# Two chained attentions on one core: PSUM as one eight-bank tile, the end of the second attention on pairs of units, and another order of instructions

## The chip, the core and the metric

The kernel runs on one core of a Trainium2 chip. The metric is device time in microseconds (us), the median of several runs. A core has TensorE (PE, matrix products, with weight loads shown apart as PEld), VectorE (DVE), ScalarE (ACT), GpSimd (POOL) and SyncE (SP, which here issues every transfer). Each engine runs its own instructions in the order in which the program issued them and waits on semaphores for the others. Matmul results land in PSUM, eight banks of 512 fp32 values in each of 128 partitions; inputs and other results live in SBUF.

## The reference

The first attention has 4 batches, 8 heads, 768 positions and a head size of 64, with a bias by distance; a query sees the first 8 keys and the last 96. Its output, (4, 768, 512), is the input x of a second layer: four experts, each a causal attention of head size 64 on all 768 positions, two of which are chosen per token and weighted.

```python
scores = scale * q @ k.T                       # 1 / sqrt(64)
keep = (pos_k < 8) | (0 <= pos_q - pos_k < 96)
scores = where(keep, scores - slope[h] * dist, -1e9)
x = softmax(scores) @ v                        # heads side by side: (4, 768, 512)

logits = x @ w_gate                            # (4, 768, 4)
topk = the 2 largest; w = exp(their logits); w /= w.sum()
for e in range(4):
    a = softmax(causal(scale * (x @ wq[e]) @ (x @ wk[e]).T))
    out += w[e if chosen else 0] * (a @ (x @ wv[e]) @ wo[e])
```

## The kernel before

The work is cut into 24 units: unit u is 128 positions, number ri = u % 6 of batch u // 6. Positions are loaded for two units at once (q and k, 512 KB each) and for one unit (v, 256 KB). The steps of a unit have short names, which a table called `ORDER` lists in the order in which they are issued; it is the order on every engine, SP included. In the table `s0-5:0` is step s0 of unit 5 in PSUM slot 0, and a star picks the second of the engines that a step may run on.

The steps of the first attention: `ldq`, `ldk`, `ldv` load (SP). `cq`, `ck`, `cv` cast to fp16 (POOL, for the first unit ACT and DVE). `tq`, `tk` transpose (PE, L591 and L596) and `eq`, `ek` copy the result to SBUF (DVE). `s0`, `s1` are the scores of four heads each, transposed (PE, L630); `x0`, `x1` their exponentials (ACT, L634), 1024 elements to a partition, or 512 for the first unit of a batch; `m0`, `m1` the product with the stored factors M of bias and mask (DVE, L639). `z0`, `z1` multiply by V (PE, L647 and L650), with a column of ones in V that gives the sum of each row; `r0`, `r1` are its reciprocals (DVE, L661), and `n0`, `n1` the normalised rows in fp16 (DVE, L663). The first eight positions of a batch are copied into each unit's blocks by `kp` (POOL) and `vp` (an SP transfer that waits for z0 and z1).

Then come the projections: `tx`, `ex` transpose x (PE L679, DVE), `pq` multiplies by wq and wk (PE, L689) and `eqk` copies out (DVE or ACT), `pv` multiplies by wv and w_gate (PE, L695), `ev` copies the values out (ACT or DVE). The routing: `xr` is the exponential of the logits (ACT, L708), `mx` the sorted largest (DVE, L711), `wr` keeps those of the two chosen experts and sums them (DVE, L712), `zi` is the reciprocal of the sum (DVE, L715).

The second attention: `s20`, `s21`, `s22` scores (PE, L727) and `x20` to `x22` exponentials (ACT, L731), in parts of up to four blocks; `af` cuts the diagonal block (POOL, L739). Its end, called for each unit: `y2` multiplies by the values (PE, L751); `rz` takes the reciprocals of the sums (DVE, L757); `cw` multiplies weights, `zi` and `rz` (DVE, L758); `n2` scales (DVE, L761); `tz`, `ez` transpose (PE L769, DVE); `po` multiplies by wo (PE, L774); `eo` copies out (ACT or DVE); `so` stores (SP, L783). L384 is the copy helper of all casts and copies.

PSUM is cut into named slots: two of two banks each for scores, `s0` and `s1`, and four of one bank, `w0` to `w3`, for all else. SBUF buffers are rings: three for blocks of q and k, four units for the rest. The weights are loaded once (`ld-q`, `ld-k`, `ld-v`, `ld-o`, 512 KB each, and `ld-g`, 8 KB) and cast (`w-q` and so on). `warm` runs 24 matmuls on zeros at the start. At the end `good0` to `good2` test that all sums are in range, `total` adds the tests up on PE, `flag` copies the count out, and a branch on it, with `hint` just ahead of it, leads to a general path that these inputs don't take.

Of the kernel before, what the change touches and what calls it, by code (L numbers as in the profile page):

```python
# [8 lines left out]
F32 = mybir.dt.float32  # L9
# [7 lines left out]
P = 128  # L17
N_G, N_L = 8, 96
N_WARM = 24

ORDER = """
ident nil ldq-0 warm:2 ldk-0 ident32 ldq-2 dg ldk-2 iota d mask ldv-0 d0 d1 M-1-1 ldq-4 cq-0 ck-0
ld-k M-0-0 M-1-0 tk-0:3 cq-2 tq-0:1 ek-0 ld-q M-0-1 V1one* eq-0 tq-2:2 perm kg-0 s0-0:1 ldv-1 eq-2
s1-0:0 ck-2 x0-0 x1-0 m0-0 kp-0 V2one ld-g s0-1:1 m1-0 s1-1:0 tk-2:3 x1-1 kp-1 cv-0 ek-2 vg-0 z1-0:2
x0-1 r1-0 s0-2:0 n1-0 cq-4 z0-0:0 x0-2 r0-0 vp-0 m1-1 tq-4:1 ld-v m0-2 n0-0 eq-4 ldk-4 tx-0:0 w-q*
s1-2:1 ldv-2 kp-2 w-k* cv-1 w-g ex-0 z1-1:1 m0-1 x1-2 r1-1 z0-1:3 pq-0:0 m1-2 vp-1 w-v* ldv-3 r0-1
n1-1 s1-3:1 ldq-6 n0-1 x1-3 eqk-0 tx-1:3 pv-0:2 ld-o ck-4 s20-0:0 xr-0 mx-0 s0-3:1 ex-1 x20-0 ev-0*
x0-3 wr-0 cv-2 tk-4:3 kp-3 z0-2:0 ek-4 af-0 zi-0 m0-3 y2-0:2 z1-2:1 s0-4:0 cv-3 vp-2 r1-2 r0-2
s1-4:1 rz-0 x0-4 ldk-6 pv-1:3 cw-0 kp-4 n2-0 ldq-8 n0-2 pq-1:2 x1-4 cq-6 n1-2 ldv-6 ones mx-1 ldk-8
m1-3 eqk-1* tq-6:1 tx-2:0 m1-4 w-o z0-3:2 ex-2 s20-1:1 r0-3 s0-5:0 m0-4 pq-2:0 xr-1 x0-5 wr-1 eq-6  # L30
ck-6 ev-1 n0-3 s1-5:0 eqk-2* z1-3:2 x20-1 vp-3 m0-5 tk-6:1 ldv-4 r1-3 tz-0:0 x1-5 pv-2:3 ldk-10 ek-6
af-1 n1-3 kg-6 s0-6:1 s1-6:0 ez-0 x0-6 m1-5 tx-3:2 po-0:0 x1-6 ldq-10 kp-6 m0-6 y2-1:1 ldq-12 xr-2
eo-0 cq-8 ex-3 s21-2:1 s0-7:0 rz-1 x21-2 mx-2 pq-3:2 zi-1 ldv-7 cw-1 x0-7 cv-6 ev-2* wr-2 tq-8:0
ck-8 n2-1 eqk-3* s1-7:1 eq-8 s20-2:0 x1-7 z0-6:1 tz-1:3 m1-6 tk-8:2 cv-4 r0-6 ez-1 x20-2 z1-6:0 n0-6
s20-3:1 vg-6 r1-6 z1-4:1 n1-6 po-1:3 ck-10 vp-6 ek-8 ldv-5 s21-3:0 eo-1 r1-4 tx-6:0 n1-4 pv-3:2
x20-3 kp-7 ex-6 z0-4:3 m0-7 tk-10:1 xr-3 ev-3 vp-4 cq-10 pq-6:0 r0-4 x21-3 n0-4 ek-10 tx-4:3 af-2
zi-2 ldk-12 mx-3 s0-8:1 ex-4 s1-8:0 cq-12 ldq-14 x0-8 eqk-6 pq-4:3 m1-7 so-1 tq-12:1 eqk-4* cv-7
wr-3 tq-10:0 eq-12 x1-8 s21-4:1 eq-10 cv-5 z0-7:1 z1-7:2 x21-4 r0-7 kp-8 s20-4:0 m1-8 vp-7 z0-5:0
ldv-8 z1-5:3 x20-4 r1-7 n0-7 s22-4:1 r0-5 n1-7 y2-2:1 ck-12 r1-5 x22-4 n0-5 tx-7:2 ldk-14 n1-5
s1-9:0 s20-6:1 rz-2 tx-5:3 x20-6 cw-2 ldv-9 ex-7 tk-12:0 ldq-16 x1-9 ex-5 cq-14 s0-9:1 ek-12 pq-5:2  # L40
x0-9 zi-3 n2-2 kp-9 af-4 pv-5:3 eqk-5* m0-8 s0-10:1 tq-14:1 xr-5 af-3 mx-5 x0-10 wr-5 pq-7:2 cv-8
eq-14 ev-5 m1-9 s21-5:0 eqk-7* s1-10:1 m0-10 z1-8:3 x21-5 z0-8:1 kp-10 r1-8 tz-2:2 kg-12 y2-3:0
ck-14 r0-8 vp-8 ez-2 x1-10 n1-8 ldv-10 pv-4:2 rz-3 n0-8 ldk-16 po-2:3 cw-3 ldv-12 cv-9 tx-8:1 n2-3
eo-2 s22-5:0 so-0 ex-8 s1-11:1 xr-4 ev-4 m0-9 tz-3:0 tk-14:3 x22-5 cq-16 mx-4 pq-8:1 ez-3 ek-14
x1-11 m1-10 s1-12:0 po-3:0 x1-12 af-6 eqk-8 z1-9:3 eo-3 s0-12:1 m1-12 s20-5:0 x0-12 wr-4 z0-9:1
pv-6:0 ck-16 zi-4 x20-5 r1-9 vp-9 r0-9 n1-9 y2-4:2 ldq-18 zi-5 n0-9 xr-6 so-2 ev-6 s21-8:1 rz-4
s0-11:0 af-5 mx-6 ldk-18 x21-8 wr-6 tx-9:3 tq-16:1 cw-4 ldv-11 x0-11 kp-12 ex-9 cv-10 tk-16:0 n2-4
eq-16 s20-8:1 ldv-13 s20-7:0 x20-8 m1-11 tz-4:2 pq-9:3 ez-4 ek-16 x20-7 af-8 z0-10:1 po-4:2 m0-11
eqk-9* y2-5:0 cq-18 r0-10 eo-4 n0-10 s1-13:1 rz-5 s21-9:0 cw-5 x1-13 cv-12 z1-10:1 n2-5 tq-18:2
vp-10 r1-10 m0-12 tz-5:3 x21-9 z1-12:0 ldq-20 n1-10 s0-13:1 ez-5 so-3 pv-7:1 kp-13 eq-18 ck-18 x0-13  # L50
ldk-20 po-5:3 r1-12 mx-7 ev-7* tx-10:2 xr-7 s1-14:0 zi-6 eo-5 wr-7 s0-14:1 vg-12 x1-14 zi-7 z0-12:1
ex-10 tk-18:3 af-7 vp-12 r0-12 n1-12 pq-10:2 so-5 cv-11 x0-14 ek-18 so-4 m1-13 s20-9:0 eqk-10*
z0-11:0 kg-18 n0-12 cv-13 pv-8:3 x20-9 r0-11 n0-11 tx-12:1 kp-14 z1-11:2 cq-20 mx-8 ex-12 y2-6:0
ldv-14 xr-8 s21-10:1 ev-8 rz-6 r1-11 s0-15:0 wr-8 x21-10 n1-11 y2-7:1 pq-12:3 rz-7 cw-6 cw-7 x0-15
n2-6 n2-7 tx-11:2 tq-20:0 m0-13 eqk-12* tz-7:1 s22-10:1 ex-11 s1-15:0 x22-10 ez-7 z1-13:3 kp-15
eq-20 z0-13:2 ck-20 x1-15 tz-6:1 vp-13 s1-16:1 r1-13 ez-6 n1-13 pq-11:0 ldv-15 x1-16 m0-14 ldq-22
ldv-16 po-7:1 cv-14 r0-13 eqk-11* n0-13 po-6:3 m1-14 eo-7 s21-11:0 s22-11:1 eo-6* x21-11 pv-9:1
m0-15 tx-13:2 so-6 z0-14:0 x22-11 mx-9 s0-16:0 r0-14 ex-13 pv-10:3 kp-16 n0-14 af-9 xr-9 x0-16
z1-14:2 wr-9 y2-8:0 ev-10* cv-15 vp-14 s20-10:1 r1-14 mx-10 ev-9 ldk-22 zi-8 n1-14 s1-17:0 xr-10
x20-10 ldv-19 zi-9 tk-20:1 rz-8 wr-10 so-7 cw-8 pq-13:2 m1-15 x1-17 af-10 n2-8 y2-9:3 ek-20 cq-22  # L60
eqk-13* tz-8:0 s20-11:0 ez-8 s1-18:1 rz-9 x20-11 tx-14:1 cw-9 cv-16 po-8:0 ex-14 z0-15:2 n2-9 x1-18
z1-15:1 r0-15 ck-22 tz-9:3 n0-15 eo-8 vp-15 s20-12:0 s0-17:1 r1-15 ez-9 pq-14:2 n1-15 so-8 x0-17
zi-10 m1-16 ldv-18 tq-22:3 x20-12 m0-16 po-9:0 eqk-14* m1-18 tk-22:1 eq-22 eo-9 s0-18:0 s20-13:1
m1-17 so-9 x0-18 z0-16:2 pv-11:3 ldv-17 x20-13 kp-18 ek-22 af-12 y2-10:0 mx-11 r0-16 xr-11 ev-11
cv-18 s21-14:0 wr-11 s20-14:1 x21-14 n0-16 tx-15:1 vg-18 ldv-22 z1-16:3 rz-10 x20-14 ex-15 s1-19:0
vp-16 r1-16 cw-10 pv-12:2 n1-16 x1-19 n2-10 s0-19:1 mx-12 m0-18 tx-16:3 tz-10:0 kp-19 pq-15:1 x0-19
m0-17 ez-10 ex-16 ev-12 s1-20:0 xr-12 eqk-15 s0-20:1 x1-20 po-10:0 kp-20 m1-19 z0-18:3 pq-16:1 cv-17
x0-20 wr-12 eo-10* af-14 z1-17:2 eqk-16* r0-18 so-10 s1-21:1 n0-18 af-11 s0-21:0 ldv-20 r1-17 x1-21
z0-17:3 n1-17 cv-19 z1-18:1 zi-11 y2-12:0 r0-17 y2-11:2 r1-18 vp-18 af-13 n0-17 x0-21 ldv-23 zi-12
rz-12 n1-18 kp-21 s21-15:1 rz-11 cw-12 pv-13:1 cw-11 x21-15 n2-12 tx-17:3 n2-11 tz-12:0 mx-13  # L70
s21-16:0 ev-13 ex-17 s20-15:1 xr-13 x21-16 ez-12 pq-17:3 wr-13 m0-19 x20-15 cv-20 tz-11:0 z1-19:2
ez-11 po-12:1 r1-19 m0-21 eqk-17* po-11:0 af-15 zi-13 eo-12 s22-16:0 n1-19 s20-16:1 eo-11* z0-19:3
x22-16 so-12 y2-13:1 cv-22 pv-14:2 r0-19 x20-16 so-11 rz-13 n0-19 tx-18:0 vp-19 cw-13 mx-14 s1-22:0
n2-13 xr-14 ldv-21 ev-14 s21-17:1 ex-18 x1-22 tz-13:3 tx-19:1 wr-14 pq-18:0 ez-13 m0-20 x21-17 m1-20
pv-15:3 y2-14:2 xr-15 ex-19 eqk-18* s22-17:1 zi-14 rz-14 s20-17:0 mx-15 cw-14 ev-15 wr-15 z0-20:1
x22-17 n2-14 z1-20:0 po-13:3 r0-20 r1-20 vp-20 n0-20 y2-15:2 zi-15 eo-13 n1-20 tz-14:1 rz-15 x20-17
s0-22:1 m1-21 so-13 pv-16:0 kp-22 cw-15 pq-19:3 cv-23 ez-14 xr-16 n2-15 ev-16 x0-22 cv-21 mx-16
wr-16 po-14:2 m1-22 tx-20:1 eqk-19* z1-21:0 af-17 ex-20 s0-23:1 eo-14 r1-21 s1-23:0 m0-22 z0-21:1
x1-23 tz-15:3 af-16 n1-21 pq-20:2 vp-21 r0-21 ez-15 so-14 n0-21 x0-23 pv-17:0 m1-23 tx-21:3 eqk-20*
po-15:1 ex-21 xr-17 s20-19:0 ev-17 eo-15* s20-18:1 z1-22:3 x20-18 z0-22:2 mx-17 so-15 wr-17 y2-16:1  # L80
x20-19 zi-16 vp-22 r1-22 r0-22 pq-21:0 rz-16 n0-22 cw-16 n2-16 s20-20:0 eqk-21* n1-22 s21-20:1
pv-18:1 x21-20 tx-22:2 mx-18 y2-17:3 xr-18 zi-17 x20-20 ex-22 wr-18 z1-23:0 rz-17 ev-18 s21-21:1
cw-17 af-20 r1-23 s20-21:0 zi-18 n2-17 x21-21 tz-16:1 pq-22:2 n1-23 af-19 ez-16 m0-23 tz-17:1
pv-19:0 eqk-22* af-18 ez-17 po-16:3 xr-19 mx-19 x20-21 ev-19* z0-23:2 wr-19 po-17:1 r0-23 n0-23
y2-18:0 eo-16 s20-22:1 rz-18 s21-22:0 cw-18 eo-17 zi-19 so-16 tx-23:2 n2-18 pv-20:3 x21-22 so-17
ex-23 y2-19:1 mx-20 tz-18:2 pq-23:0 rz-19 x20-22 cw-19 ez-18 n2-19 pv-21:2 xr-20 eqk-23* af-22 wr-20
po-18:1 mx-21 ev-21* ev-20 af-21 s22-22:0 xr-21 eo-18* s21-23:1 x22-22 pv-22:3 wr-21 x21-23 so-18
y2-20:0 y2-21:2 rz-20 zi-20 zi-21 xr-22 mx-22 ev-22 cw-20 s20-23:0 wr-22 s22-23:1 rz-21 x20-23 n2-20
# [773 lines left out]
```

## Time and profile before

| | us |
|---|---|
| device time, median of 3 runs (lowest to highest) | 146.87 (146.66 to 147.22) |
| the profiled execution's device time | 146.58 |
| its span, first to last instruction | 144.9 |
| PE, DVE, ACT, POOL busy | 130.0, 120.2, 120.1, 70.2 |
| mean granted PE clock, 1 being full speed | 0.964 |
| share of the DMA engines' time taken by the data queue | 72.2% |

A profile gives one execution. In its slices the span is cut into 40 equal parts and each digit is a busy share in tenths, 9 being 90% or more. A group of instructions has its count, its busy time, the mean of one in ns, and the engine's idle time ahead of it with what ended that. A wait has the time in total, how often, and the longest. Matmuls overlap in PE's pipeline, so a mean of one is far longer than the distance from one to the next.

### The profile page before, as it was taken

To read this page: it belongs to the slowest core of one execution; us is meant where nothing else is said; L and a number is where in the kernel's file an instruction comes from. 1 tells how busy PE (TensorE), PEld (TensorE's weight loads), DVE (VectorE), ACT (ScalarE), POOL (GpSimd) and SP (SyncE) were. 2 spreads that over 40 slices of the span, in tenths; PEclk is the share of its full clock that TensorE was granted. 3 is DMA by queue.
4 is the path that set the end of the run, shared out by engine and by line. 5 is a ranking of instruction groups with operands and counts; after the bars stand their busy time and mean duration, and the time that the engine had idled before them with its cause. 6 is when DMAs were issued, how large, how long until landed. Compare 5 with 4: busy or idle time off the path is not lost.

```text
span 144.9 us, 5515 instructions
## 1 busy us (share of the span) xinstructions
PE 130.0 (90%) x2222; PEld 101.5 (70%) x2222; DVE 120.2 (83%) x420; ACT 120.1 (83%) x198; POOL 70.2 (48%) x116
## 2 busy tenths in 40 slices
PE   6985779697998999999999999889999999999870
PEld 2453466485877788778798787668878887978620
DVE  1257784897999989999999998989999998887870
ACT  3867766679985998988999998889999998899760
POOL 6058216534997596674773345545641370413100
PEclk9999555999999999999999999999999999999999
DMA  2999999599898997969999699770527204023164
GB/s 78 304 275 305 245 310 222 177 299 246 226 289 181 294 273 166 246 147 299 202 258 303 148 253 261 212 175 9 157 67 219 73 14 152 5 75 113 34 235 140
DMA packets 55725, 27.83 MB, mean 192 GB/s; under 512 B 26096, under 2 KB 52368, under 8 KB 55696
## 3 DMA queue, kind: packets, MB, share of 16 engines
q1 hardware_dynamic: 55696, 27.45, 72.2%
q8 instruction: 18, 0.29, 0.9%
q14 instruction: 11, 0.09, 0.2%
HBM read 20.98 MB, written 6.29 MB: 188 GB/s over the span
## 4 chain that ended last, share of the span: by engine, by line
PE 60%; DVE 14%; DMA 8%; SPq 7%; issue 3%; ACT 2%; POOL 2%; ACTq 0%
PE pq L689 13%; PE s L727 7%; PE sc L630 7%; PE pv L695 6%; PE z L647 5%; PE z L751 5%; DMA wg<-in_moe_w_gate_dram 5%; PE po L774 4%; SPq L578 4%; DMA rawqk<-in_k_dram 4%; PE tx L679 3%; PE tk L596 3%; DVE A L639 3%; PE z L650 3%; PE tq L591 3%
## 5 line engine op out<-in xcount | busy, mean ns | idle before, releaser
L634 ACT ACTIVATE A<-sc 128x1024 f16<-128x1024 f32 (+1 forms) x48 | 44.6, 960 | 6.7 <-PE sc L630 6.3
L731 ACT ACTIVATE A<-s 128x1024 f16<-128x1024 f32 (+1 forms) x48 | 43.4, 930 | 2.1 <-PE s L727 1.8
L639 DVE TENSOR_TENSOR A<-A,M 128x1024 f16<-128x1024 f16 (+1 forms) x48 | 35.0, 742 | 0.2 <-ACT A L634 0.2
L739 POOL TENSOR_SCALAR_AFFINE_SELECT A<-A 128x512 f16<-128x512 f16 x24 | 18.0, 761 | 19.6 <-ACT A L731 14.1
L689 PE MATMUL pq<-xT,wqk 128*128 128x128 f16 x384 | 26.3, 223 | 1.3 <-DVE z L761 1.2
L689 PEld LDWEIGHTS <-wqk 128*128 128x128 f16 x384 | 23.1, 100 | 2.3 <-DVE z L761 1.5
L384 POOL CAST k<-rawqk 128x1024 f16<-128x1024 f32 x11 | 15.3, 1388 | 12.7 <-DMA rawqk<-in_k_dram 12.6
L663 DVE TENSOR_TENSOR x<-z,rall 128x256 f16<-128x256 f32 x48 | 19.5, 413 | 0.4
L630 PE MATMUL sc<-qT,kT 64*128 64x128 f16 x352 | 17.4, 224 | 2.5 <-DVE kT L384 1.2
L647 PE MATMUL z<-V,A 128*128 128x65 f16 x192 | 17.1, 196 | 2.2 <-POOL V L384 1.0
L384 POOL CAST V<-rawv 128x512 f16<-128x512 f32 x24 | 15.7, 658 | 3.9 <-PE s L727 1.9
L647 PEld LDWEIGHTS <-A 128*128 128x128 f16 x192 | 13.1, 99 | 5.1 <-DVE wr L712 0.8
L727 PE MATMUL s<-QK 64*128 64x128 f16 x336 | 15.9, 219 | 0.0
L384 POOL COPY kT<-KG 128x32 f16<-128x32 f16 x20 | 5.4, 272 | 20.9 <-PE sc L630 20.9
L695 PE MATMUL pv<-wvg,xT 128*128 128x264 f16 x96 | 15.3, 283 | 0.0
L630 PEld LDWEIGHTS <-kT 64*128 64x128 f16 x352 | 11.1, 97 | 5.9 <-issue 1.9
L384 POOL CAST q<-rawqk 128x1024 f16<-128x1024 f32 x11 | 11.7, 1059 | 6.7 <-DMA rawqk<-in_q_dram 6.7
L650 PE MATMUL z<-V,A 128*128 128x65 f16 x160 | 14.6, 195 | 0.0
L384 ACT CAST QK<-pq 128x512 f16<-128x512 f32 x20 | 11.9, 595 | 2.5 <-PE pq L689 2.5
L774 PE MATMUL po<-wo,zT 128*128 128x512 f16 x48 | 13.9, 380 | 0.0
L751 PE MATMUL z<-V,A 128*128 128x65 f16 x336 | 13.8, 193 | 0.0
L751 PEld LDWEIGHTS <-A 128*128 128x128 f16 x336 | 12.3, 97 | 1.8 <-issue 0.4
(70 smaller groups left out, 226.0 us busy)
## 6 DMA issues: line engine op xcount, KB each, us to landing
rawqk<-in_q_dram SPq DMA_DIRECT2D x12, 512.0 KB
rawqk<-in_k_dram SPq DMA_DIRECT2D x12, 512.0 KB
rawv<-in_v_dram SPq DMA_DIRECT2D x24, 256.0 KB
out_dram<-o_sb SPq DMA_DIRECT2D x24, 256.0 KB
w<-in_moe_wk_dram SPq DMA_DIRECT2D x1, 512.0 KB
w<-in_moe_wq_dram SPq DMA_DIRECT2D x1, 512.0 KB
w<-in_moe_wv_dram SPq DMA_DIRECT2D x1, 512.0 KB
wo<-in_moe_wo_dram SPq DMA_DIRECT2D x1, 512.0 KB
```

The source lines that it names most:

```text
L384: act.copy(o, i) if e == "ACT" else (dve if e == "DVE" else pool).tensor_copy(o, i)
L630: mm(sc[:, par, pr, prev * P:(prev + 1) * P], lhsT=share(kT, u - prev)[L, p, :], rhs=share(qT, u)[L, p, :], start=True, stop=True)
L634: act.activation(A1[(2 * u + hf) % (2 * R)][:, :, :, 0:w], T.pop(("s", u, hf))[:, :, :, 0:w], func=Exp, scale=scale1)
L639: eng[e].tensor_tensor(a, a, M[:, hf, :, :, :] if ri else M0[:, hf, :, :, :], op=Alu.mult)
L647: mm(z[:, h % 4, :], lhsT=a[:, par, pr, 0:P], rhs=V1[i][:, h, 0:DV], start=True, stop=not ri)
L663: add(f"n{hf}", lambda e, hf=hf, r1=r1: dve.tensor_tensor(x16[i][:, 256 * hf:256 * hf + 256].rearrange("p (h d) -> p h d", d=Dh), T.pop((" ...
L689: mm(ps[:, j, :], lhsT=wqk[:, ko, j, :], rhs=xT[i][:, ko, :], start=(ko == 0), stop=(ko == nko - 1))
L695: mm(ps[:, :], lhsT=xT[i][:, ko, :], rhs=wvg[:, ko, :], start=(ko == 0), stop=(ko == nko - 1))
L727: mm(sc[:, par, n, :], lhsT=QK2[b % 2][L, ki, 2 + p2, :], rhs=QK2[b % 2][L, ri, p2, :], start=True, stop=True)
L731: act.activation(A2[i][:, :, 4 * ch:4 * ch + m, :], T.pop(("s2", u, ch))[:, :, 0:m, :], func=Exp, scale=scale2)
L751: mm(z[:, ex, :], lhsT=A2[i][:, ex % 2, n, :], rhs=V2[b % 2][:, ki, ex, 0:DV], start=(j == 0), stop=(j == len(mine) - 1))
L774: mm(ps[:, :], lhsT=zT[i][:, p2, :], rhs=wo[:, p2, :], start=(p2 == 0), stop=(p2 == E // 2 - 1))
```

## The change

Five things are different.

1. PSUM is one tile of eight banks. Any step may take any bank, and a step that needs two takes two that adjoin (`s0-1:01`).
2. `z0` and `z1` become one step `z` of 16 (for the first unit of a batch 8) matmuls into two banks, with one `r` of eight reciprocals and one `n` of 512 elements.
3. The end of the second attention, from `y2` to `ez`, and `zi`, run once for two units; units 22 and 23 go singly. `po`, `eo` and `so` stay by unit.
4. The routing weights are divided by their sum in a step of their own, `wn`, once for two units, so that `cw` is a plain product.
5. The table is another one. A number behind a plus sign (`s0-1:01+21`) puts that many matmuls on zeros ahead of the step: 21, 10, 1 and 6 of them, all ahead of unit 5's scores. Four more `ev` and `w-k` run on DVE and not on ACT, `V1one` on DVE and not on POOL. The loads begin with k0, q0, q2, k2, the gate weight, k4, v0, q4, v2, v1, and only then wk, wq, q6, wv; before, they began with q0, k0, q2, k2, v0, q4, wk, wq, v1, gate weight, wv. `hint` and the tests stand further ahead in the last lines.

```diff
-ident nil ldq-0 warm:2 ldk-0 ident32 ldq-2 dg ldk-2 iota d mask ldv-0 d0 d1 M-1-1 ldq-4 cq-0 ck-0
-ld-k M-0-0 M-1-0 tk-0:3 cq-2 tq-0:1 ek-0 ld-q M-0-1 V1one* eq-0 tq-2:2 perm kg-0 s0-0:1 ldv-1 eq-2
...
+ident ldk-0 V1one nil ldq-0 dg warm:4 ldq-2 iota d mask ident32 d1 perm M-1-0 ldk-2 ck-0 d0 ld-g
+cq-0 M-1-1 tk-0:3 ldk-4 tq-0:5 cq-2 ek-0 eq-0 s0-0:45 s1-0:23 ldv-0 x1-0 ck-2 ldq-4 M-0-1 w-g tq-2:3
+x0-0 m1-0 M-0-0 kg-0 eq-2 kp-0 ldv-2 s0-1:01+21 tk-2:3 ck-4 x0-1 s1-1:67 ek-2 ldv-1 x1-1 m0-0 kp-1
...
+    banks = psum.tile([P, 8, 4 * P], F32, name="banks")
+    def busy(t):
+        for n in range(st.idle):
+            mm(t[:, 0:P], lhsT=nil[:, 0:P], rhs=nil[:, 0:P], start=True, stop=True)
...
+    def two():
+        lo, hi = st.slots
+        assert hi == lo + 1
+        busy(banks[:, lo, :])
+        return banks[:, lo:hi + 1, :]
...
+    groups = [[u, u + 1] for u in range(0, NU - 2, 2)] + [[NU - 2], [NU - 1]]
...
+        def z1(e):
+            T["z", u] = z = two()[:, :, 0:4 * DV].rearrange("l f (h d) -> l f h d", d=DV)
+            for h in range(H):
...
+        add("r", lambda e: dve.reciprocal(r1, T["z", u][:, :, :, Dh]), {"DVE": 0.11}, ["z"])
+        add("n", lambda e: dve.tensor_tensor(
+            x16[i][:, :].rearrange("p (f h d) -> p f h d", f=2, d=Dh), T.pop(("z", u))[:, :, :, 0:Dh],
+            r1.unsqueeze(3).to_broadcast([P, 2, 4, Dh]), op=Alu.mult), {"DVE": 0.61}, ["r", ("tx", u - R)])
...
+        add("wn", lambda e: dve.tensor_tensor(
+            wn, wn, zi[:, us[0]:u + 1].unsqueeze(2).to_broadcast([P, nu, E]), op=Alu.mult), {"DVE": 0.1}, ["zi"],
+            port=True)
+        add("rz", lambda e: dve.reciprocal(r2, T["z2", u][:, :, :, Hd]), {"DVE": 0.07 + 0.02 * nu}, ["y2"])
+        add("cw", lambda e: dve.tensor_tensor(cw_, wn, r2, op=Alu.mult), {"DVE": 0.1},
+            ["rz", "wn", *[("n2", w) for w in had[-1:]]], port=True)
+        add("n2", lambda e: dve.tensor_tensor(z_, T.pop(("z2", u))[:, :, :, 0:Hd],
+                                              cw_.unsqueeze(3).to_broadcast([P, nu, E, Hd]), op=Alu.mult),
+            {"DVE": 0.065 + 0.27 * nu}, ["cw", *[("tz", w) for w in had[-1:]]])
```

## The prediction

> **What bounds it now.** I read the page's busy line, the slices, windows of four stages, the groups by shape, the waits and the chain that ended last.
>
> First, the page's busy line and the slices of ACT and of PE's clock.
>
> ```profile
> PE 130.0 (90%) x2222; PEld 101.5 (70%) x2222; DVE 120.2 (83%) x420; ACT 120.1 (83%) x198; POOL 70.2 (48%) x116
> ...
> ACT  3867766679985998988999998889999998899760
> ...
> PEclk9999555999999999999999999999999999999999
> ```
>
> PE looks like the bound at 90%, and the chain is 60% PE. But the busy time is a union of pipelined matmuls: a pq matmul is recorded at 223 ns while sixteen take 0.89 us of the chain, 56 ns each. Priced by such spacings (pq 0.89, pv 0.45, two sc of 0.22, tx 0.22, po 0.43, z 16 x 30 ns, s and y2 14 matmuls of 29 ns each, and so on) a unit needs about 4.3 us of PE, 24 units 102 us: 70% of the span. VectorE (DVE) and ScalarE (ACT), whose busy time is real work, have 83% each. The windows by stage say where the other 17% is:
>
> ```profile
> 10.00:30.00 20.00, 14.65 (x197) 11.13 (x196) 14.76 (x42) 12.60 (x16) 9.57 (x17) 0.74 0.97 253
> 30.00:130.00 100.00, 97.35 (x1837) 79.90 (x1835) 93.44 (x324) 92.35 (x148) 54.92 (x78) 1.00 0.73 185
> 130.00:144.90 14.90, 9.91 (x162) 6.66 (x158) 8.95 (x50) 8.80 (x18) 1.86 (x3) 0.99 0.37 137
> ```
>
> The columns are length, then PE, PEld, DVE, ACT, POOL busy, PE clock, DMA share, GB/s. From 30 to 130 us DVE is 93% and ACT 92% busy: the two together are the bound there. ACT's idle 24.8 us are 3.6 before 10 us, 7.4 from 10 to 30, 7.65 from 30 to 130 and 6.1 after. From 10 to 30 the clock averages 0.74 and the DMA engines are full. What ended ACT's idle times, from the waits:
>
> ```profile
> ACT A L634 <- PE sc L630: 6.3, 7, 1.3
> ACT M L473 <- DVE d L483: 2.1, 1, 2.1
> ACT QK L384 <- PE pq L689: 2.5, 5, 1.1
> ACT A L731 <- PE s L727: 1.8, 6, 0.4
> ACT wvg L384 <- DMA w<-in_moe_wv_dram: 1.3, 1, 1.3
> ```
>
> The largest is ACT waiting for first-attention scores (L634); by the timeline 4.5 of these 6.3 us lie before 36 us. The prices come from the groups by shape (count, then busy us and mean ns):
>
> ```profile
> L663 DVE TENSOR_TENSOR x<-z,rall 128x256 f16<-128x256 f32 x48 | 19.5, 413 | 0.4
> L384 DVE COPY xT<-tx 128x512 f16<-128x512 f16 x24 | 9.9, 414 | 0.4 <-PE tx L679 0.2
> L761 DVE TENSOR_TENSOR z<-z,cw 128x256 f16<-128x256 f32 x24 | 9.8, 416 | 0.2
> L661 DVE RECIPROCAL rall<-z 128x4 f32<-128x4 f32 x48 | 7.8, 171 | 0.5 <-PE z L647 0.2
> L384 DVE COPY zT<-tz 128x256 f16<-128x256 f16 x24 | 6.7, 280 | 0.3 <-PE tz L769 0.3
> L758 DVE SCALAR_TENSOR_TENSOR cw<-wr,zi,rall 128x4 f32<-128x4 f32 x24 | 6.3, 269 | 0.3
> L715 DVE RECIPROCAL zi<-zall 128x1 f32<-128x1 f32 x24 | 3.5, 151 | 0.1
> L384 DVE COPY o_sb<-po 128x512 f32<-128x512 f32 x5 | 3.4, 686 | 0.0
> L795 DVE SCALAR_TENSOR_TENSOR ge<-zall,ge 128x24 f32<-128x24 f32 x1 | 0.2, 183 | 0.0
> L384 ACT CAST V<-pv 128x256 f16<-128x256 f32 x17 | 6.5, 380 | 0.2 <-DVE mx L711 0.2
> ```
>
> DVE from PSUM costs 413 ns for 256 fp32 elements and 686 for 512: about 1.07 ns an element and 140 fixed. A four-element reciprocal is 171, nearly all fixed. So each merged pair saves one fixed part.
>
> **DVE, step by step.** n0 and n1 become one n of 512: 48 x 0.413 = 19.8 becomes 24 x 0.686 = 16.5, saves 3.3. r0 and r1 become one r of 8 elements: 48 x 0.171 becomes 24 x 0.175, saves 4.0. The end of second attention runs in 13 groups (11 pairs, 2 single units) in place of 24: rz 24 to 13 of 0.175, saves 1.9; zi 24 to 13 of 0.151, 1.7; n2 from 24 x 0.416 to 11 x 0.686 + 2 x 0.416, 1.6; ez from 24 x 0.280 to 11 x 0.414 + 2 x 0.280, 1.6. cw (24 x 0.269) becomes 13 cw and 13 wn, plain multiplies of up to 8 elements that the trace lacks; bounds are the zi row (0.151) and the ge row of L795 (0.183); I take 0.16 as they are nearest to zi, which saves 2.3 (2.5 to 1.7). Together 16.4. Back come four more ev on DVE (11 for 7, 0.41 each, 1.6), w-k (moved from ACT; 0.77 to 1.05 by the two casts of 1024, I take 0.8) and V1one (moved from POOL, 0.3). DVE: 120.2 - 16.4 + 2.7 = 106.5 us.
>
> **ACT** loses those four ev (4 x 0.380) and w-k (1.04): 120.1 - 2.6 = 117.5 us. It alone is now the fullest engine. DVE's saving therefore does not shorten the kernel by itself: of 16.4 us, 2.6 pass to ACT through moved work, the rest only makes what ACT waits for come earlier. So the sum is ACT's work plus ACT's idle.
>
> **PE** gets 38 filler matmuls of 128 columns (21, 10, 1, 6), at 56 ns 2.1 us, all before unit 5's scores, where PE is idle 3.9 of the 10 us from 10 to 20 in the windows; nothing else is added or removed. If PE were the bound it would cost the 2.1 us. The other additions wait: y2 of a pair waits for both units' x2 and af, so rz, cw, n2, tz and po of the first unit come one unit (about 5 us) later. Behind them queue only the stores (so, on SP), and wanted back are A2 and o_sb, rings of four units; I price it at nothing, and at up to 0.6 (one po evacuation) a pair where a ring runs out, 7 us in all. vp on SP waited for z0 and z1 and now for z, the same moment; the loads behind it on SP are no worse off.
>
> **Order of the first 30 us.** Rows of the timeline: both halves of the first block landed at 6.9 us, the first score exponential began at 10.72. k0 now comes first and is cast on DVE while q0 is still landing, so after q0 only one cast (1.03), one transpose (0.6), one copy (0.69) and the scores remain: about 9.7. The eight M of 128x128 (1.8 in all, in their row) now come after it, so ACT's idle before 10 us stays 3.6. The load queue then brings k4, v0, q4, v2, v1 before any expert weight; the gate weight, which landed at 18.05 behind 1.5 MB (a 6.63 us piece of the chain), goes ahead of them. Up to wq's end the queue holds 5.0 MB, of which 1.05 have landed at 6.9; the other 3.95 at the 290 GB/s of the 5 to 15 us windows take 13.6, so wq lands near 20.5. ACT meanwhile has two x of 0.6, ten of 1.0 (units 0 to 5) and 1.8 of M: 13 us from 9.7 to 22.7. So the weights no longer make ACT wait, and I halve the 7.4 us of idle to 3.7 (bounds: 1.5, one longest wait here and there; 7.4, nothing gained).
>
> From 30 to 130 I take 6.0 for 7.65, since DVE, which delivers to the matmuls that ACT waits for, is now 9% less loaded than ACT (bounds 4.0 and 7.65). The tail keeps its 6.1: last stores and flag were issued together (141.05 and 141.10), with 3.76 us of ending behind them, so the earlier flag is worth nothing.
>
> Sum: 117.5 + 3.6 + 3.7 + 6.0 + 6.1 = 136.9 us span. The profiled run took 146.58 for a span of 144.9, 1.7 outside; the median of the runs is 0.29 above that run. Forecast 136.9 + 1.7 + 0.3 = **138.9 us**.
>
> **Two rules beside the rows.** The clock first: the windows show 0.50 from 15 to 25 us, after 5 us in which PE started only 52 matmuls. The Trainium skill (TensorE: Matmul & The Clock Gate, Part 1) says that the clock is released by a busy window of about 3.4 us and lost after an idle one; The change's largest filler, 21 matmuls or 1.2 us, is a third of such a window, and the page doesn't say that a third is enough. By the rule taken strictly the clock falls again and the sum is that of the third rival.
> Against the merges: rows show a half of z holding one PSUM bank for 0.24 + 0.17 + 0.41 = 0.82 us; merged, two banks are held 0.48 + 0.18 + 0.69 = 1.35. The skill (Perfetto Trace Analysis, Matmuls) wants independent matmul groups rotated through banks so that one is evacuated while the next computes; by it the merge gives up that overlap, and the second rival would be the sum. No run so far shows what is given up.
>
> **Rivals.** *ACT keeps its idle.* All of DVE's saving ends in DVE's idle, the new order fills nothing: 117.5 + 24.8 = 142.3, or 144.3 us. For it: most ACT waits were ended by PE, not DVE. Against: DVE was as full as ACT for 100 us, and PE's inputs come from it. 20%.
> *Banks run short, slower.* z and y2 of a pair each take two adjoining banks until their last DVE read, from the same eight that the scores use in twos; scores come late and ACT starves. Price: the extra 0.53 us of hold, once in every second unit, on top of the kept idle: 142.3 + 12 x 0.53 = 148.7, or 150.7 us. It decides from 2.6 us of added ACT waits on top of the kept idle, 0.11 us a unit. Against: score exponentials hold 2 banks for about 1.4 us, four times a unit, some 11 of the 40 bank-us of a 5 us unit; everything together stays near 23. 10%.
> *The fillers don't hold the clock.* PE stays at 0.5 for 10 us again, ACT's waits for sc remain: the 10 to 30 idle stays 7.4, 140.6 span, 142.6 us. 15%.
> The forecast case has 55%. Its own range goes from the lower bounds, 117.5 + 3.6 + 1.5 + 4.0 + 6.1 = 132.7 (134.7 us), to 5.5 for 10 to 30 and 7.65 for 30 to 130, 140.4 (142.4 us).
>
> **How the numbers follow.** 0.5% (0.7 us) is about what a measurement of this kernel can tell from no change; the three runs spread over 0.56. The range reaches over the forecast case, the first rival (a few tenths above it for overruns) and the third: 134.7 to 145.0. Faster needs under 146.1: 0.55 + 0.20 + 0.15, less 0.04 for overruns of the first rival by over 1.8 us: 0.86. Those 0.04 are the chance of no change, and the second rival's 0.10 that of slower.
>
> **What would show it.** DVE near 106.5, ACT near 117.5 us; n near 0.69, r 0.175, wn and cw near 0.16; ACT's idle from 10 to 30 halved, PEclk without a run of 5s. Wrong: n at 0.8 or more (the two-bank read is not one instruction's fixed cost), ACT waits for sc or s longer than 8.1 together, or ACT under 80% busy.

## The result and the profile after

The changed kernel takes **154.75 us** (median of 4 runs, 154.16 to 156.22) beside 146.76 (146.00 to 147.22) for the kernel before: 5.6% slower, ratio 1.0564 with a 95% interval of 1.0475 to 1.0654. Forecast were 138.9 us and a range of 134.7 to 145.0. Ratios here leave disturbed runs out, so one can differ a little from that of the medians beside it; the ratio is then the one to go by.

The page's busy line, and the slices of ACT and of PE's clock, after:

```profile
PE 132.8 (87%) x2260; PEld 105.2 (69%) x2260; DVE 117.5 (77%) x339; ACT 118.4 (78%) x193; POOL 68.6 (45%) x112
...
ACT  3559776786954898968989999899999976899630
...
PEclk9999995699995999999999999999999999999995
```

The span is 152.4 us. DVE executes 81 instructions fewer and is busy only 2.7 us less (117.5 for 120.2). ACT has 1.7 us less to do and stands for 34.0 us in place of 24.8. The clock still falls, later than before (slices 7 and 8, then slice 13). The windows by stage (length; PE, PEld, DVE, ACT, POOL busy; clock; DMA share; GB/s):

```profile
0.00:10.00 10.00, 8.07 (x36) 3.80 (x37) 2.89 (x11) 4.90 (x10) 3.88 (x15) 1.00 0.88 221
10.00:30.00 20.00, 15.20 (x237) 12.97 (x237) 14.75 (x27) 14.64 (x24) 11.05 (x15) 0.83 1.07 258
30.00:130.00 100.00, 94.30 (x1745) 77.27 (x1741) 87.14 (x247) 85.22 (x136) 50.63 (x77) 0.98 0.68 177
130.00:152.40 22.40, 15.23 (x254) 11.11 (x248) 12.69 (x56) 13.69 (x24) 3.09 (x5) 0.91 0.33 121
```

ACT's idle time is 5.1, 5.4, 14.8 and 8.7 us in the four stages; before it was 3.6, 7.4, 7.65 and 6.1. Most of the loss lies between 30 and 130 us. The stages are cut by time and not by work: the last one, 22.4 us long in place of 14.9, holds work that the kernel before had done by 130 us. From the waits, first those of ACT, then two of PE:

```profile
ACT A L650 <- PE banks L646: 8.9, 10, 3.8
ACT o_sb L394 <- PE banks L807: 3.6, 6, 1.1
ACT QK L394 <- PE banks L700: 3.1, 4, 1.7
ACT A L741 <- PE banks L737: 2.4, 7, 0.7
...
PE banks L646 <- ACT A L650: 3.0, 4, 1.2
PE banks L690 <- DVE x L675: 2.8, 2, 2.5
```

The first line is the old largest wait (scores for the first attention's exponentials), grown from 6.3 to 8.9. With the fourth, for the second attention's scores, it makes 11.3 us, over the 8.1 that the prediction named as a sign of being wrong; so is ACT's 78%, under 80%. The fifth tells something new. L646 are the score matmuls: they need nothing that an exponential (L650) makes. What they wait for is the PSUM bank that it still reads. With three short waits of that kind in other PE steps it makes 4.1 us. Before, the whole of it was one line:

```profile
PE sc L630 <- ACT A L634: 0.6, 1, 0.6
```

The groups by shape that the prediction had priced:

```profile
L675 DVE TENSOR_TENSOR x<-banks,rall 128x512 f16<-128x512 f32 x24 | 16.5, 688 | 0.5
L789 DVE TENSOR_TENSOR z<-banks,cw 128x512 f16<-128x512 f32 x11 | 7.6, 688 | 0.2
L655 DVE TENSOR_TENSOR A<-A,M 128x512 f16<-128x512 f16 x8 | 5.2, 664 | 0.4 <-ACT M L483 0.4
L674 DVE RECIPROCAL rall<-banks 128x8 f32<-128x8 f32 x24 | 4.8, 200 | 5.1 <-PE banks L668 4.4 <-PE banks L666 0.7
L783 DVE TENSOR_TENSOR wr<-wr,zi 128x8 f32<-128x8 f32 x11 | 3.0, 277 | 0.1
L786 DVE RECIPROCAL rall<-banks 128x8 f32<-128x8 f32 x11 | 2.2, 198 | 1.1 <-PE banks L772 1.1
L787 DVE TENSOR_TENSOR cw<-wr,rall 128x8 f32<-128x8 f32 x11 | 2.0, 183 | 0.2
```

n and n2 (688) are as priced (686). wn is 277 for 160, cw 183, r 200 for 175, and the half-size m, which the change doesn't touch, 664 for 470.

### The profile page after: what moved, and what is told of

It reads as the page before. It is cut to its first block, busy times and chain, and to the rows that moved or that the text cites. A ratio compares the mean times of both kernels' runs of the same rounds, so it can differ in the third digit from the quotient of the medians.

```text
span 152.4 us, 5547 instructions
## 1 busy us (share of the span) xinstructions
PE 132.8 (87%) x2260; PEld 105.2 (69%) x2260; DVE 117.5 (77%) x339; ACT 118.4 (78%) x193; POOL 68.6 (45%) x112
## 4 chain that ended last, share of the span: by engine, by line
PE 65%; DVE 18%; ACT 6%; issue 3%; DMA 2%; POOL 1%; DVEq 0%; ACTq 0%; POOLq 0%
PE banks L700 13%; PE banks L646 7%; PE banks L706 7%; PE banks L807 6%; DVE A L655 5%; PE banks L737 5%; PE banks L772 5%; PE banks L503 5%; PE banks L666 4%; PE banks L690 3%; PE banks L607 3%; DVE x L675 3%; ACT A L741 3%; PE banks L668 3%; PE banks L612 2%
## 5 line engine op out<-in xcount | busy, mean ns | idle before, releaser
L650 ACT ACTIVATE A<-banks 128x1024 f16<-128x1024 f32 (+1 forms) x48 | 45.0, 961 | 9.3 <-PE banks L646 8.9
L741 ACT ACTIVATE A<-banks 128x1024 f16<-128x1024 f32 (+1 forms) x48 | 42.4, 923 | 5.4 <-PE banks L737 2.4
L700 PE MATMUL banks<-xT,wqk 128*128 128x128 f16 x384 | 27.5, 229 | 0.1
L646 PE MATMUL banks<-qT,kT 64*128 64x128 f16 x352 | 17.8, 223 | 4.3 <-ACT A L650 3.0
L646 PEld LDWEIGHTS <-kT 64*128 64x128 f16 x352 | 11.4, 96 | 8.8 <-issue 6.0
L675 DVE TENSOR_TENSOR x<-banks,rall 128x512 f16<-128x512 f32 x24 | 16.5, 688 | 0.5
L737 PE MATMUL banks<-QK 64*128 64x128 f16 x336 | 15.4, 218 | 0.5 <-DVE qT L394 0.5
L706 PE MATMUL banks<-wvg,xT 128*128 128x264 f16 x96 | 14.7, 282 | 0.8 <-DVE x L675 0.7
L666 PE MATMUL banks<-V,A 128*128 128x65 f16 x192 | 14.8, 196 | 0.6 <-DVE z L789 0.3
L394 ACT CAST QK<-banks 128x512 f16<-128x512 f32 x20 | 12.0, 600 | 3.3 <-PE banks L700 3.1
L807 PE MATMUL banks<-wo,zT 128*128 128x512 f16 x48 | 13.9, 380 | 0.8 <-DVE zT L394 0.6
L666 PEld LDWEIGHTS <-A 128*128 128x128 f16 x192 | 12.5, 99 | 1.8 <-ACT A L741 0.3
```

The lines of the kernel that those rows point to most:

```text
L394: act.copy(o, i) if e == "ACT" else (dve if e == "DVE" else pool).tensor_copy(o, i)
L646: mm(sc[:, par, pr, prev * P:(prev + 1) * P], lhsT=share(kT, u - prev)[L, p, :], rhs=share(qT, u)[L, p, :], start=True, stop=True)
L650: act.activation(A1[(2 * u + hf) % (2 * R)][:, :, :, 0:w], T.pop(("s", u, hf))[:, :, :, 0:w], func=Exp, scale=scale1)
L666: mm(z[:, h // 4, h % 4, :], lhsT=a[:, 0:P], rhs=V1[i][:, h, 0:DV], start=True, stop=not ri)
L675: add("n", lambda e: dve.tensor_tensor(x16[i][:, :].rearrange("p (f h d) -> p f h d", f=2, d=Dh), T.pop(("z", u))[:, :, :, 0:Dh], r1.unsqu ...
L700: mm(ps[:, j, :], lhsT=wqk[:, ko, j, :], rhs=xT[i][:, ko, :], start=(ko == 0), stop=(ko == nko - 1))
```

## Experiments

The theories. *Banks*: the numbers of the PSUM banks make PE wait. *Place*: a merged step must stand where its later half stands, and what waited for the earlier half comes late. *Plan*: the new order of the steps is worse whatever the steps are. *Merging*: the long steps lose by themselves. In the expectations, theory O is the plan and theory M the merging with its two banks.

### The tile alone

```diff
-    def wtile(shape, dt, name):
-        return psum.tile(shape, dt, name=name, tag=f"w{st.slots[0]}")
+    banks = psum.tile([P, 8, 4 * P], F32, name="banks")
```

Old order, old steps, the slots written as bank numbers.

> Order, steps and engines of before; only PSUM is the one tile of eight banks (scores in banks 0 to 3, all else in 4 to 7, just as the slots were). Theory O, that the new order table costs the time and the merges do not: as before, 146.0 to 147.6 us. Theory M, that steps which hold two banks and come later starve ACT: also as before, since nothing is merged here. A third possibility, that one tile for all banks brings waits of its own: 149 us or more.

Measured: 146.55 us, ratio 1.0013 (0.9972 to 1.0055). One tile in place of six names costs nothing.

### Order and merging crossed

```diff
-... z1-0:6 x0-1 r1-0 s0-2:01 n1-0 cq-4 z0-0:4 x0-2 r0-0 ... n0-0
+... x0-1 s0-2:45 cq-4 z-0:23 x0-2 r-0 ... n-0       # old order, all merges
-... z-0:67 x0-2 ... r-0 ... n-0
+... z0-0 z1-0 x0-2 ... r0-0 r1-0 ... n0-0 n1-0      # new order, no merges
```

A moved or split step needs bank numbers; here they came from a rule: the free bank whose last reader stands earliest in the order. Where units are paired in the old order, the ring of A2 has six buffers in place of four, so that the first unit's exponentials are kept.

> Before's order with all of the change's merged steps: one z, r, n per unit, the end of the second attention on pairs, wn; each merged step stands where the later of its two parts stood, banks are given out anew, no filler matmuls, engines and loads as before. The ring A2 has six buffers in place of four, because a pair's y2 comes one unit later. Theory O: 142 to 146 us, DVE's real work falling by about 8 us. Theory M: 150 to 156 us, with ACT waiting longer for scores (over 12 us in the waits of the two score lines, against 8.1).

Measured: 158.47 us, 1.0800 (1.0715 to 1.0885).

> The change's order with nothing merged: z, r, n by halves, the end of the second attention by single units, weights and sums in one instruction as before; each part stands where the merged step stands; one tile, fillers, loads and engines of the change. Theory O: 155 to 162 us, slower still than the change, since the merges at least saved DVE's work. Theory M: 150 us or less.

Measured: 164.16 us, 1.1195 (1.1120 to 1.1270). Each order is worse with the other's steps, by 12 and by 9 us. Read alone, that says that the new order is the bad part. It took a later control to see that the rule for the banks was part of both numbers.

```diff
-s0-0:45 s1-0:23 ... s0-1:01+21        # the changed kernel, 
+s0-0, s1-0, s0-1 ... by the rule      # the same order but for s20-18 and s20-22
```

> The change as it is, but each step takes the bank, or the adjoining pair, that has been free longest in the issue order (219 of the bank numbers are others). If reusing a bank too soon costs the time (the scores of units 2 to 4 all go through banks 0 and 1, and ACT waits 0.49 us after each): 150 to 153 us, and no row of 0.49 us waits at 18 to 22 us. Theory O with the engine queues' order as the cause, and not the banks: 153.5 to 156 us.

Measured: 156.73 us, 1.0567 (1.0456 to 1.0678), by the ratio the same as the changed kernel. Besides the numbers, two score steps stand one or two places from where they stood. I took it that banks don't matter. What it shows is only that the rule's numbers are no better than the kernel's.

### Which merge, and merging or moving

All four in the old order, with banks by the rule.

```diff
-z1-u ... z0-u     r1-u ... r0-u     n1-u ... n0-u
+z-u               r-u               n-u                # half merge
+z1-u z0-u         r1-u r0-u         n1-u n0-u          # halves moved
```

> The kernel before on one PSUM tile and in its old order, only the two halves of z, r and n merged into one each, at the place of the later half. old_order_all_merges took 158.5 us, so the merges cost 11.8 us in that order. If the longer way from z to tx carries it (0.30 us a unit, 24 units: up to 7.2 us), this one takes 151 to 154; if the pairs carry it all, it stays within 1 us of 146.8.

Measured: 154.81 us, 1.0565 (1.0481 to 1.0648).

> The kernel before on one PSUM tile, no step merged: only the earlier half of z, of r and of n is moved in the order to directly before the later half, the places that the merged steps had in old_order_half_merge (154.8 us, 8.3 over before). If the place is what costs, this takes 153 us or more, since two halves have two fixed parts where the merged step has one (24 x 0.12 us of DVE). If the merging itself costs (one long step, two banks held at once), it stays within 1.5 us of 146.5.

Measured: 153.61 us, 1.0472 (1.0435 to 1.0510).

```diff
-y2-0 ... tz-0 ... po-0 ... y2-1 ... tz-1 ... po-1
+y2-1 (both units) ... tz-1 ... po-0 po-1               # pairs only
+y2-0 y2-1 ... tz-0 tz-1 ... po-0 po-1                  # units moved
```

> The kernel before on one PSUM tile and in its old order, only y2 to ez on pairs of units, at the place of the later unit, without wn, with rings of six for A2 so that the first unit's exponentials are kept. The rest of the 11.8 us of old_order_all_merges: if the two kinds of merging cost separately, 151 to 155 us, and with old_order_half_merge the two excesses sum to about 11.8; if each alone is covered by slack that only both together use up, both stay under 149.

Measured: 157.47 us, 1.0702 (1.0592 to 1.0812).

> The kernel before on one PSUM tile with rings of six for A2, no step merged: only y2, rz, zi, cw, n2, tz, ez, po, eo and so of every even unit moved in the order to directly before those of the odd unit, the places that they had in old_order_pairs_only (157.5 us, 11 over before). If the place costs: 157 us or more. If the joining itself costs (nothing of the first unit is released before the second is done): under 150.

Measured: 157.73 us, 1.0761 (1.0715 to 1.0807). Steps that only stand at the merged places cost nearly what the merged ones cost: 153.6 to 154.8, and 157.7 to 157.5. Joining itself is worth about 1 us either way. And the two kinds don't add up: 8 and 11 alone, 12 together. Each of the four has bank numbers of its own by the rule, which can be a part of each figure.

### The longest stall, mended

The timeline of the changed kernel, DVE, then POOL, then PE, around ACT's longest stand (3.85 us, to 47.69):

```profile
40.71 1.60 DVE L655 TENSOR_TENSOR A<-A,M 128x512 f16<-128x512 f16 x2
42.23 1.13 DVE L783 TENSOR_TENSOR wr<-wr,zi 128x8 f32<-128x8 f32 x1
43.29 0.19 DVE L786 RECIPROCAL rall<-banks 128x8 f32<-128x8 f32 x1
43.41 0.15 DVE L674 RECIPROCAL rall<-banks 128x8 f32<-128x8 f32 x1
43.52 0.41 DVE L787 TENSOR_TENSOR cw<-wr,rall 128x8 f32<-128x8 f32 x1
43.84 0.68 DVE L675 TENSOR_TENSOR x<-banks,rall 128x512 f16<-128x512 f32 x1
...
41.99 0.80 POOL L394 COPY VG<-V 8x528 f16<-8x528 f16 x1
42.74 1.16 POOL L394 CAST V<-rawv 128x512 f16<-128x512 f32 x2
...
44.58 0.42 PE L690 MATMUL banks<-perm,x 128*128 128x128 f16 x4 [2.49 <-DVE x L675]
```

PE stands 2.49 us ahead of tx-4 for n-4 (L675), which stands on DVE behind the end of the first pair, wn-1 among it: 8 elements in 1.13 us.

```diff
-z-4:01 w-o m0-6 s20-3:67 wn-1 vp-4 rz-1 r-4 s0-8:45 cw-1 cv-6 n-4
+z-4:01 r-4 n-4 w-o m0-6 s20-3:67 wn-1 vp-4 rz-1 s0-8:45 cw-1 cv-6
```

> The changed kernel with two words of its order moved: r-4 and n-4 stand directly behind z-4, ahead of m0-6, wn-1, rz-1 and cw-1, on DVE; nothing else changes. If PE's stand of 2.49 us before tx-4 comes from what is queued ahead of n-4 on DVE (0.85 + 1.13 + 0.19 + 0.4 us), tx-4 starts near 42.2 in place of 44.6, ACT's stand of 3.85 us falls to under 1.5, the clock keeps 1.0 at 46 to 50 us and the time falls by 2 to 4 us, to 151 to 153. If that stall is only the place where slack that is lost anyway comes out, the time stays within 0.7 us of 154.8 and a stall of the same size stands later.

Measured: 154.72 us, 1.0503 (1.0450 to 1.0556), no gain. tx-4 did start at 42.44. From that kernel's timeline and waits:

```profile
42.44 0.41 PE L690 MATMUL banks<-perm,x 128*128 128x128 f16 x4 [0.48 <-DVE x L675]
44.80 0.40 PE L798 MATMUL banks<-ident,z 128*128 128x128 f16 x4 [1.95 <-DVE z L789]
...
ACT A L650 <- PE banks L646: 8.3, 10, 3.4
```

PE now stands at its next step, tz-1, for the end of the same pair, and ACT's longest wait is 3.4 in place of 3.8. The wait moved one instruction down the queue. The clock still falls to 0.5 there, from 46.0 to 49.4 us, as in the changed kernel (46.2 to 49.6).

### The fillers

```diff
-s0-1:01+21 ... s1-2:01+10 ... z-1:67+1 ... s1-5:45+6
+s0-1:01 ... s1-2:01 ... z-1:67 ... s1-5:45
```

> The changed kernel without its 38 filler matmuls. If the fillers hold the clock for part of the first 30 us, PEclk falls earlier than 22 us and the time rises by 1 us or more (10 us at 0.5 delay what PE has to do there). If they do nothing that the order doesn't do, the time stays within 0.7 us of 154.8 or falls by up to the 2.1 us that they take on PE.

Measured: 152.83 us, 1.0375 (1.0334 to 1.0416), 1.9 us less than the changed kernel by the medians. But the seven runs are of two kinds. Four had a mean granted clock of 0.98 and took 151.9 to 152.8 us; three had 0.93 and took 154.6 to 155.7, as long as the changed kernel, whose four runs had 0.94 to 0.96. The profile is of one of the three; its clock, and its window from 10 to 30 us:

```profile
PEclk9997555599999999999999999999999999999995
...
10.00:30.00 20.00, 14.30 (x171) 11.20 (x169) 15.34 (x28) 13.14 (x22) 9.95 (x14) 0.59 0.96 230
```

In it the clock is 0.5 from 13.8 to 30.8 us, with the fillers from 22.3 to 29.1. So the fillers' 2.1 us on PE are not shown to be what the 1.9 are: the slow stretch of this execution is some 10 us longer than with them, and the faster runs without them go with a higher clock. What sets the clock of a run is not shown.

### The banks' numbers alone

```diff
-tk-4:7 kp-3 z0-2:4 ek-4 af-0 zi-0 m0-3 y2-0:6      # old: scores 01 and 23, all else 4 to 7
+tk-4, z0-2, y2-0 and all others by the rule         # old order, old steps
```

> A control that the earlier runs lacked. The steps and the order of the kernel before on one PSUM tile, and only the bank numbers changed, to those of the rule that gave banks in old_order_all_merges, new_order_no_merges and in all the runs with moved or merged steps: the free bank, or pair of banks, whose last reader stands earliest in the order (one step, s1-4, one place later for it). In the old table the scores have four banks to themselves, in twos, and all other tiles the other four; the rule mixes them. Theory 'banks': PE, which goes through its steps in order, waits for a bank that ACT or DVE still reads, and the time rises by 3 to 6 us over 146.5; then that much of what the runs in the old order lost is not the merges' doing. Theory 'place of the steps': within 1 us of 146.5.

Measured: 150.00 us, 1.0262 (1.0156 to 1.0369). The rule costs 3.4 us where, but for one step moved by one place, nothing else is changed, so the runs above in the old order are to be read against 150.0: the half merge costs 4.8, the pairs 7.5, both 8.5, if the rule costs them as much.

```diff
-s0-8:45 ... z-6:67 ... y2-1:23        # 133 of 268 numbers changed by a search,
+s0-8:23 ... z-6:67 ... y2-1:67        # not one word of the order moved
```

The search took queues in order and costs from the traces, and kept the numbers for which PE waits least.

> The changed kernel, its order untouched word for word, with only the bank numbers of 133 of 268 tiles changed: searched for short waits on banks, with the start-to-start costs of the traces. new_order_other_banks had other banks too, but by the rule, and no better ones. In the changed kernel's trace PE waits 3.9 us in score steps (L646) for ACT to leave a bank, 2.7 more than before. Theory 'banks': these go and the time falls by 2 to 4 us, to 151 to 153. Theory 'place of the steps' or 'the new order is the worse plan': within 1 us of 154.75.

Measured: **149.78 us**, 1.0273 (1.0158 to 1.0388): 5.0 us less than the changed kernel. Its wait of scores for ACT's banks, and its window from 30 to 130 us:

```profile
PE banks L646 <- ACT A L650: 0.5, 2, 0.3
...
30.00:130.00 100.00, 95.61 (x1808) 78.34 (x1805) 88.91 (x253) 87.78 (x138) 53.26 (x80) 1.00 0.71 182
```

3.0 us of that wait became 0.5, ACT's idle in the stage 12.2 for 14.8, and the clock has no drop there (1.00 for 0.98). From 10 to 30 us ACT's idle fell as well, 3.2 for 5.4, where the clock is 0.91 for 0.83. All four runs had a higher mean clock, 0.97 to 0.99 for 0.94 to 0.96. A part of the 5.0 us goes with that; whether the banks held the clock up is not shown. The one run with the changed kernel's own numbers and its fillers at such a clock (0.98, in new_order_one_stall_mended) took 153.2, still 3.4 more.

> new_order_no_merges (164.2 us) with only the bank numbers searched, nothing else. Theory 'banks': most of its 9.4 us over the changed kernel were banks, two singles per merged step taken by the rule; it falls by 8 us or more, to 156 or less, and stands within 4 us of new_order_searched_banks. Theory 'merges save that much in the new order': stays over 160.

Measured: 154.80 us, 1.0628 (1.0479 to 1.0777): 9.4 less than with the rule's numbers.

> old_order_all_merges (158.5 us) with only the bank numbers searched. Theory 'banks': falls by 4 to 7 us, to 152 to 154, and what is left over 146.5, some 6 us, is the merged steps' own cost in that order. Theory 'place of the steps': stays over 157.

Measured: 155.82 us, 1.0659 (1.0508 to 1.0809): 2.7 less than with the rule's.

### Order and banks searched for each kind of steps

```diff
-ORDER = """ ident ldk-0 V1one nil ldq-0 ... """
+ORDER = """ ... """                     # the same steps; order, banks and choice of engine found by
+                                         # trying moves against queues in order
```

> The changed kernel's steps and tiles to the letter (merged z, r, n; pairs; wn; the 38 fillers), under a third order table, which I searched myself with costs per step taken from the two traces as the distance between starts of queued instructions (n 0.61, r 0.115, n of a half 0.33, score exponential 0.91) and not from the row means. Theory 'only the table is bad': with a table that fits the merged steps ACT's idle from 30 to 130 us falls from 14.8 to under 8 and the time to 147 or below, at best near 140. Theory 'merged steps are the loss' (a unit's tx waits 0.30 us longer for its normalised output: r + n 0.88 after the last z in place of 0.58): no table takes the 24 x 0.30 = 7.2 us out, and it stays over 151.

Measured: 152.38 us, 1.0337 (1.0243 to 1.0432).

> The steps of the kernel before (halves of z, single units at the end of second attention) on the one PSUM tile, with the 38 fillers, under an order that I searched in the same way and with the same effort as for merged_steps_own_search. Theory 'only the table is bad', merges worth nothing either way: within 2 us of merged_steps_own_search. Theory 'merged steps are the loss': shorter than merged_steps_own_search by 5 us or more. If the 7 us of DVE time that the merges save (start to start: 24 x 0.054 for n, 24 x 0.069 for r, and 11 x about 0.3 for the pairs) were worth its whole length, it would be longer by up to 7.

Measured: 151.40 us, 1.0353 (1.0250 to 1.0456). No difference, but both poor. The busy line and the two m groups of the merged one show one reason:

```profile
PE 134.4 (89%) x2260; PEld 101.3 (67%) x2260; DVE 124.8 (82%) x340; ACT 117.3 (77%) x190; POOL 69.5 (46%) x114
...
L655 DVE TENSOR_TENSOR A<-A,M 128x1024 f16<-128x1024 f16 x40 | 32.2, 821 | 0.0
L655 DVE TENSOR_TENSOR A<-A,M 128x512 f16<-128x512 f16 x8 | 6.5, 821 | 0.0
```

DVE is 7.3 us busier than in the changed kernel with one instruction more; the two m groups (777 and 664 there) take 2.7 us of that, and wn and cw lengthen in the same way where they run beside POOL. The other reason is PE, told at the end. With both costs in the search and no fillers, the merged steps were searched once more from new_order_searched_banks on, and the single ones from the old order:

> The changed kernel's steps (merged z, r, n; pairs; wn), without fillers, under an order and bank numbers searched once more from new_order_searched_banks on, now with three costs that the traces show and the first search lacked: 95 ns each time that PE goes from 128-row matmuls to scores of 64 rows or back (29 to 123 and 53 to 148 ns to the next start), m, wn and cw on DVE and POOL's steps never at the same time, and waits on banks. Theory 'order and banks are the cause, the merges are nearly free': 147 or below, perhaps under 143. Theory 'the merged steps lose by themselves': above merged steps in the old order with searched banks less what a free order gives, 150 or more.

Measured: **147.86 us**, 1.0090 (1.0062 to 1.0117).

> The steps of the kernel before on one PSUM tile, without fillers, searched in the same way and for the same number of moves as merged_steps_second_search, from the old order on. If the merges are worth their DVE time from start to start (some 7 us of DVE at most): up to 3 us longer than merged_steps_second_search. If they cost: shorter by 2 us or more. If they are nearly free: within 2 us, both under 147.

Measured: 148.56 us, 1.0145 (1.0105 to 1.0186). With the same number of moves for both, though from different starts, the merged steps are 0.7 us shorter by the medians, less than surely told apart, as the intervals overlap. What the second search mended is not known step by step: PE's changes fell (162 to 102 and 176 to 114 in the records), but the large m did not get faster (864 ns merged, 855 single; 797 in the kernel before). None of the eighteen beats the kernel before.

| us | single steps | merged steps |
|---|---|---|
| old order; its own, the rule's, searched banks | 146.6; 150.0; not run | none; 158.5; 155.8 |
| new order; its own, the rule's, searched banks | none; 164.2; 154.8 | **154.75**; 156.7; 149.8 |
| order and banks searched, second time | 148.6 | 147.9 |

## Why the prediction was wrong

**DVE's saving, 16.4 us: mis-sized by more than half.** The instructions fell as counted and the row means were right. But means can't be subtracted one from another. Five successive lines of DVE in the kernel before (start, duration):

```profile
62.62 0.16 DVE L715 RECIPROCAL zi<-zall 128x1 f32<-128x1 f32 x1
62.70 0.23 DVE L661 RECIPROCAL rall<-z 128x4 f32<-128x4 f32 x2
62.90 0.42 DVE L663 TENSOR_TENSOR x<-z,rall 128x256 f16<-128x256 f32 x1
63.24 0.15 DVE L715 RECIPROCAL zi<-zall 128x1 f32<-128x1 f32 x1
63.31 0.41 DVE L663 TENSOR_TENSOR x<-z,rall 128x256 f16<-128x256 f32 x1
```

n begins at 62.90, lasts 0.42, and the next instruction begins at 63.24: 0.08 before n's end. zi lasts 0.15 and holds the queue for 0.07. Taken from start to start, in queued stretches, n0 and n1 are 0.331 each (413 in the row), one n 0.608 (688), a reciprocal of four 0.092 (171), of eight 0.115 (200). The fixed part of n by this measure is 0.054 us. A pair of n then saves 0.054 us, not 0.14, a pair of r 0.069, not 0.167. All merges together: n 1.3, r 1.7, rz 0.8, zi 0.7, n2 0.7, ez 0.8, cw and wn 1.3, so 7.2 us. From 120.2, with 2.7 of moved work, that gives 115.7; the slower half-size m (1.5) and wn (1.3), less 0.6 for the faster full m, make 117.9, and 117.5 was measured. The Trainium skill (Perfetto Trace Analysis, Optimizing Scalar/DVE Operations) says that a profiled latency is about twice the engine's fixed cost, since the second half overlaps with the next instruction; the rows agree (0.08 of r's 0.17 is overlap), and my 140 ns "fixed" part was read from such latencies.

This step is wrong, yet not the cause of the loss: less saved is still saved.

**ACT's work, 117.5: right** (118.4).

**ACT's idle time: the step that failed.** I let it fall to 19.4 us; it rose to 34.0. The sentence "From 30 to 130 I take 6.0 for 7.65, since DVE ... is now 9% less loaded than ACT (bounds 4.0 and 7.65)" had no upper bound above the time of before, as if a new order could only keep or cut the waits. It was 14.8. The prediction took DVE's load to set when scores come. The waits show PE's queue there, and ahead of the scores in it a bank that is not free (4.1 us) or a step that stands before them (2.49 us ahead of tx-4 alone).

**Banks: the right rival, refused for a wrong reason.** "Banks run short" had the mechanism, scores late for want of a bank, its mark (added ACT waits) and 10%. I set against it that 23 of 40 bank-us (banks times the us that they are held) are in use. That counts room; but a step has one bank number written into the order and waits for that bank, however many others are free. Other numbers alone gain 5.0 of the 8.0 us, with what goes with the clock. That the rival's price, 12 x 0.53 = 6.4 us by the longer hold of a merged tile, lies near is luck: unmerged steps in the new order with the rule's numbers lose still more (164.2, and 154.8 after the search). The Trainium skill's sentence on rotating matmul groups through banks (Perfetto Trace Analysis, Matmuls) did point to the place of the loss; the runs show that the numbers carry it (5.0 us) and not the merging.

**Pairing and place.** "I price it at nothing, and at up to 0.6 a pair, 7 us in all" if a ring runs out. In the old order the pairs cost 7.5 us over the 150.0 of the rule, if the rule costs as much there, and just moving the units there costs as much. No ring shows: A2 had six buffers in those runs, and every wait ahead of a copy to o_sb was ended by po, none by a store. By these runs what costs is the place, a step in an in-order queue that waits for the second unit while others stand behind it. In an order made for them the cost is gone (147.9 to 148.6).

**Fillers: not settled.** I let them vanish in PE's idle time from 10 to 20 us, though they stand in PE's queue right ahead of scores that ACT waits for; without them the kernel is 1.9 us shorter by the medians, but only in runs with a higher clock. The clock did not hold: it is 0.5 from about 22 to 29 us in place of 15 to 25 (0.83 for 0.74 in the window). That it falls again is what the strict reading of the clock rule said; the wait that the third rival put on it (7.4 us of ACT's idle) did not stay.

**The first 30 us.** The order of loads did cut ACT's idle from 10 to 30 (7.4 to 5.4, forecast 3.7). Ahead of it, "ACT's idle before 10 us stays 3.6" missed: it is 5.1, and the first exponential started at 10.90, not 9.7. **The tail** was to stay at 6.1 and is 8.7.

What is left open: of the 8.0 us, the banks' 5.0 and the fillers' 1.9 come from separate runs, both with a higher clock, and may overlap. The tail's 2.6 and the head's 1.5, the order of loads and the steps moved from ACT to DVE were not tried alone. The kernel before had no search of its bank numbers, so how much of the 5.0 such a search gives to any order isn't known. The second search says only that the loss can be had back, all but 0.9% (about 1.3 us), without undoing a merge.

## What to carry to other kernels

Price a merged instruction by the distance from its start to the next start in a queued stretch, not by the row's mean: here the means promised 2.3 times what there was. Where the order and the buffers' numbers are written out, they are part of every edit: a change that moves steps needs a control that moves them without changing them, and one that changes the bank numbers alone, or the cost of a poor table is booked to the edit. And before adding idle-time fillers or mending the longest stall, ask what stands next in the same queue, since a wait that is taken away there can appear one instruction later.

## What the runs showed of the hardware

Some DVE instructions take longer while POOL works. In the timeline above wn (8 elements, 0.16 us undisturbed) takes 1.13 us, beginning 0.24 us after POOL's copy of VG and ending after POOL's next cast has begun. In merged_steps_own_search, the 31 such instructions (m, wn, cw) with no POOL work beside them were on average under 0.01 us off their base, and 29 that shared more than 0.3 us with POOL were 0.46 longer; not each of them was, some of the large m kept their 0.68. The Trainium skill (SBUF — State Buffer, SBUF: two separate sides) calls it an exclusive lock on a shared port pair, held for a whole instruction, for DVE operations with two SBUF inputs among others; these have two, and n and ez, which read PSUM, kept their times.

PE pays about 95 ns each time it goes between matmuls of 128 rows and the scores' 64: to the next start it is 29 ns inside a z group and 123 from z to a score, 53 at the end of a score group and 148 from there to others. Counted in the records, PE changes over 114 times before, 106 after, and 162 and 176 times in the two first searches, by this estimate (56 and 62 more, 95 ns each) 5 to 6 us more for them. The Trainium skill (TensorEngine Tiling (Array Packing), Key Properties) says that a change of tiling mode drains TensorE; no run here shows whether that is what happens.
